# First x tiles in column pieces, their transposes packed into fewer PSUM tiles, merged late loads and a shorter warm-up, in a fused two-layer kernel on one core

## Chip, core and metric

The kernel runs on one core of a Trainium2 chip. The metric is device time in microseconds (us), as the median of several executions.

## The reference

```python
# B, S, D, F = 1, 2048, 576, 4608, all bf16
def reference(x, w1, b1, w2, b2):
    h = jnp.einsum("bsd,df->bsf", x, w1) + b1
    zero = jnp.zeros_like(h)
    r = jnp.where(h > zero, h, zero)
    h = r * r
    out = jnp.einsum("bsf,fd->bsd", h, w2) + b2
    return out
```

## The kernel before

x is worked off in four blocks of 512 rows. For the first layer PE needs x transposed. Blocks 1 to 3 get that from transposing DMAs; block 0 cannot wait for those, so its four row tiles (128 rows each) are loaded as they are and transposed on PE, 128 columns at a time, against an identity, into PSUM. DVE and ACT copy the results to SBUF (`xT0`). The first four output tiles of layer one are computed chunk by chunk of w1 (`part`), while the rest loads. Meanwhile PE runs a few warm-up matmuls on constants, because its clock starts at half rate (shown below).

The parts that matter (cuts marked):

```python
    wps = ps_o.tile([P, 512], FP32, name="wps", tag="po")
    WARM = [512] * 6 + [128]
    # ... one matmul for each width in WARM

    load_x(nc.sync, 0)        # a whole row tile: 128 x 576
    load_x(nc.scalar, 1)
    load_w1n(nc.sync, 0)      # w1 rows 0..127, columns 0..511
    load_x(nc.scalar, 2)
    load_w1n(nc.sync, 1)
    load_x(nc.sync, 3)
    for k in range(2, NK):
        load_w1n(nc.sync, k)
    # ... b1 and part of b2 are loaded from the gpsimd queue

    tb_po = [ps_o.tile([P, 2, HS], BF16, name="tb", tag="po") for _ in range(2)]
    tb_ph = [ps_h.tile([P, 2, HS], BF16, name="tb", tag="ph") for _ in range(4)]
    # x_transpose(j, k): one 128x128 transpose of row tile j, column chunk k,
    # each k of a half (two row tiles) into a PSUM tile of its own
    # x_copies(h): five copies of half h, on DVE and ACT in turn

    # ... in a_full(0, "k_outer"):
                for j in range(2):
                    for k in range(NK):
                        x_transpose(j, k)
                for j in range(2):
                    x_transpose(j, NK)
                x_copies(0)
                part(0, 0)
                for k in range(NK + 1):
                    x_transpose(2, k)
                part(0, 1)
                part(0, 2)
                for k in range(NK + 1):
                    x_transpose(3, k)
                x_copies(1)
                dup_windows(0)
                part(0, 3)
                part(1, 0)
                make_b1T()
                for k in range(1, NK):
                    part(1, k)
    # ... then two pairs of 64-row matmuls, and the long stage a_rows(0), which
    # takes w1 in column chunks j0..j1:
    for (j0, j1) in [(0, 1), (1, 2), (2, 4), (4, 6), (6, 8), (8, 10), (10, 12)]:
        load_w1(nc.sync, 0, j0, j1)
        load_w1(nc.sync, 1, j0, j1)
        # ...
    load_xT(1)
    for (j0, j1) in [(12, 14), (14, 16)]:
        load_w1(nc.sync, 0, j0, j1)
        load_w1(nc.sync, 1, j0, j1)
```

## Time and profile before

| | before |
|---|---|
| median at first / range | 291.28 us / 291.16 to 291.34 (3 runs) |
| span of the profiled execution | 289.6 us |
| PE busy | 285.5 us, 99% |
| opening: start of the first 64-row pair (timeline) | 9.85 us |

The first line of the profile's page for the kernel before gives busy time, share of the span and number of instructions for each engine.

```profile
PE 285.5 (99%) x2027; PEld 139.9 (48%) x2032; DVE 78.6 (27%) x176; ACT 96.7 (33%) x154; POOL 2.3 (1%) x10
```

PE is the limit, and only its opening has slack. The timeline of PE in the opening of the kernel before, with start, length, line, operation, count and, in brackets, idle time and what ended it:

```profile
2.86 0.74 PE L63 MATMUL wps<-const-bfloat16-1.0 128*128 128x512 bf16 x2
3.77 1.25 PE L149 MATMUL tb<-ident,x_sb 128*128 128x128 bf16 x10 [0.17 <-DMA x_sb<-in_x_dram]
4.87 1.01 PE L227 MATMUL pn<-xTw,w1n 128*128 128x256 bf16 x4
5.68 0.74 PE L149 MATMUL tb<-ident,x_sb 128*128 128x128 bf16 x5
6.21 1.19 PE L227 MATMUL pn<-xTw,w1n 128*128 128x256 bf16 x8
7.24 0.44 PE L149 MATMUL tb<-ident,x_sb 128*128 128x128 bf16 x5
...
9.85 0.39 PE L203 MATMUL pn<-xTw,w1n 64*128 64x512 bf16 x1
```

Two things are to be seen. First, PE waits once, 0.17 us, for x. Second, five transposes take 0.74 us at 5.68 and 0.44 at 7.24: the clock doubles in between. The records of single matmuls put the step at 6.51 us; start to start, a transpose takes 107 ns before it and 56 after, a matmul of 256 columns 213 and 109. (The record of a transpose, 311 ns in the first of these groups, is longer than the distance of starts, so records overlap; the distance is what counts.)

The table of stretches of the kernel before, for 2 to 4 and 4 to 6 us; the last two columns are the DMA engines' busy share and GB/s:

```profile
core 0: us, PE busy (x) PEld busy (x) DVE busy (x) ACT busy (x) POOL busy (x), PEclk, DMA share, GB/s
2.00:4.00 2.00, 1.83 (x8) 0.68 (x7) 0.00 (x0) 1.15 (x2) 0.70 (x2) 1.00 0.96 314
4.00:6.00 2.00, 2.00 (x18) 1.73 (x16) 0.78 (x3) 0.65 (x2) 0.18 (x1) 1.00 0.92 247
```

So 0.63 MB (314 GB/s times 2 us) arrive from 2 to 4 us, while PE warms up.

### The profile page before, as it was taken

The numbers are of one execution on the slowest core, as the hardware profiler recorded it, in microseconds if no ns is written. First come the engines' busy times: TensorE is split into PE (matmuls) and PEld (weight loads), VectorE is DVE, ScalarE is ACT, GpSimd is POOL, SyncE is SP. The second block draws the span as 40 slices with busy tenths as digits, with TensorE's granted clock in tenths as the row PEclk, the third lists the DMA queues.
The fourth block names the chain that finished last, engine by engine and source line by source line (L and its number), as shares of the span: only waits on it lengthen the run. The fifth ranks groups of instructions, "written<-read, shape, count | busy, mean of one in ns | idle before, by whom it ended". The sixth has DMA issues, their size and how long they took to land.

```text
span 289.6 us, 4693 instructions
## 1 busy us (share of the span) xinstructions
PE 285.5 (99%) x2027; PEld 139.9 (48%) x2032; DVE 78.6 (27%) x176; ACT 96.7 (33%) x154; POOL 2.3 (1%) x10
## 2 busy tenths in 40 slices
PE   8999999999999999999999999999999999999996
PEld 5544444444444555555544444444444455555555
DVE  1644554444500200000015444444440001100001
ACT  2566666666500000000027666666670000000000
POOL 3000000000000000000000000000000000000000
PEclk9999999999999999999999999999999999999999
DMA  7999999400001200000000000000000110000000
GB/s 198 221 245 188 308 389 212 92 0 2 0 14 25 52 16 18 16 16 18 16 16 2 1 2 0 2 0 2 0 2 0 36 38 16 16 16 19 33 16 18
DMA packets 31605, 16.52 MB, mean 57 GB/s; under 512 B 15700, under 2 KB 31584, under 8 KB 31584
## 3 DMA queue, kind: packets, MB, share of 16 engines
q1 hardware_dynamic: 31232, 15.91, 22.3%
q10 hardware_dynamic: 288, 0.30, 0.4%
q8 instruction: 16, 0.26, 0.4%
q14 instruction: 5, 0.04, 0.0%
q0 software_dynamic: 64, 0.01, 0.0%
HBM read 11.36 MB, written 2.36 MB: 47 GB/s over the span
## 4 chain that ended last, share of the span: by engine, by line
PE 98%; DMA 1%; issue 0%; DVE 0%
PE ph L188 42%; PE po L289 38%; PE pt L270 11%; PE pn L209 4%; PE pn L227 1%; DMA x_sb<-in_x_dram 1%; PE tb L149 1%; PE ph L190 1%; PE pn L203 1%; DVE o_sb L291 0%; PE b1T_ps L166 0%; PE pn L205 0%
## 5 line engine op out<-in xcount | busy, mean ns | idle before, releaser
L190 PE MATMUL ph<-xTw,w_h 64*128 64x512 bf16 x576 | 124.6, 376 | 0.0
L188 PE MATMUL ph<-xTw,w_h 64*128 64x512 bf16 x576 | 124.6, 376 | 0.0
L289 PE MATMUL po<-w_sb,hT 128*128 128x448 bf16 (+2 forms) x612 | 109.4, 341 | 0.0
L176 ACT ACTIVATE r<-ph,b1T 128x512 bf16<-128x512 f32 x128 | 81.1, 685 | 41.6 <-PE ph L190 41.6
L188 PEld LDWEIGHTS <-w_h 64*128 64x128 bf16 x576 | 54.1, 94 | 68.3
L289 PEld LDWEIGHTS <-hT 128*128 128x128 bf16 x612 | 58.5, 98 | 51.0
L177 DVE TENSOR_TENSOR hT<-r 128x512 bf16<-128x512 bf16 x144 | 61.2, 426 | 75.9 <-ACT r L176 75.5
L190 PEld LDWEIGHTS <-w_h 64*128 64x128 bf16 x576 | 54.1, 94 | 0.0
L291 DVE TENSOR_TENSOR o_sb<-po,b_bc 128x448 bf16<-128x448 f32 (+2 forms) x17 | 10.2, 597 | 125.8 <-PE po L289 125.8
L270 PE MATMUL pt<-hT,w_sb 128*128 128x512 bf16 x142 | 31.3, 379 | 0.1
L176 ACT ACTIVATE r<-pn,b1T 128x512 bf16<-128x512 f32 x16 | 10.3, 688 | 61.0 <-PE pn L205 59.6
L270 PEld LDWEIGHTS <-w_sb 128*128 128x128 bf16 x144 | 14.1, 98 | 17.0
L273 ACT ACTIVATE oT<-pt,b2T 128x512 bf16<-128x512 f32 x4 | 2.8, 688 | 28.3 <-PE pt L270 28.3
L209 PE MATMUL pn<-xTw,w1n 128*128 128x512 bf16 x45 | 10.4, 379 | 0.4 <-issue 0.3
L209 PEld LDWEIGHTS <-w1n 128*128 128x128 bf16 x48 | 4.5, 98 | 6.0 <-issue 0.8
L227 PE MATMUL pn<-xTw,w1n 128*128 128x256 bf16 x32 | 4.6, 295 | 0.0
L63 PE MATMUL wps<-const-bfloat16-1.0 128*128 128x512 bf16 (+1 forms) x7 | 2.8, 582 | 0.8 <-PEq L344 0.8
L227 PEld LDWEIGHTS <-w1n 128*128 128x128 bf16 x32 | 3.3, 107 | 0.5
L156 DVE COPY xTw<-tb 128x256 bf16<-128x256 bf16 x4 | 1.1, 292 | 6.7 <-PE tb L149 6.7
L119 DVE COPY xTw<-xTw 64x2048 bf16<-64x2048 bf16 x4 | 2.8, 690 | 0.2
L120 DVE COPY xTw<-xTw 64x2048 bf16<-64x2048 bf16 x4 | 2.7, 687 | 0.1
L149 PE MATMUL tb<-ident,x_sb 128*128 128x128 bf16 x20 | 2.4, 288 | 0.2 <-DMA x_sb<-in_x_dram 0.2
(23 smaller groups left out, 15.2 us busy)
## 6 DMA issues: line engine op xcount, KB each, us to landing
w_sb<-in_w_dram SPq DMA_DIRECT2D x4, 1296.0 KB, 12.7
w_h<-in_w_dram SPq DMA_DIRECT2D x14, 288.0 KB, 6.2
out_dram<-o_sb SPq DMA_DIRECT2D x15, 112.0 KB, 1.7
w_h<-in_w_dram SPq DMA_DIRECT2D x4, 144.0 KB, 3.5
w1n<-in_w_dram SPq DMA_DIRECT2D x4, 128.0 KB, 3.9
out_dram<-ot SPq DMA_DIRECT2D x4, 128.0 KB, 2.0
x_sb<-in_x_dram ACTq DMA_DIRECT2D x2, 144.0 KB, 2.9
x_sb<-in_x_dram SPq DMA_DIRECT2D x2, 144.0 KB, 3.4
```

The lines of the kernel that those rows point to most:

```text
L63: keep(nc.tensor.matmul(wps[:, 0:n], lhsT=ones[:, 0:P], rhs=ones[:, 0:n], start=True, stop=True))
L149: keep(nc.tensor.transpose(bank[:, slot, qc], xs[:, j, c0:c0 + P], ident[:]))
L176: keep(nc.scalar.activation(out=r[:], in_=bank[:], func=ACT.Relu, bias=b1T[:, ft:ft + 1], scale=1.0))
L177: keep(nc.vector.tensor_tensor(out=hTs[sb][:, ft, :], in0=r[:], in1=r[:], op=ALU.mult))
L188: keep(nc.tensor.matmul(bx[:], lhsT=w1_h[0:H, LO_C[i], jc], rhs=xT[0:H, LO_W[i], :], start=(i == 0), stop=(i == NC - 1)))
L190: keep(nc.tensor.matmul(by[:], lhsT=w1_h[H:P, UP_C[i], jc], rhs=xT[H:P, UP_W[i], :], start=(i == 0), stop=(i == NC - 1)))
L203: keep(nc.tensor.matmul(banks[2 * i][:], lhsT=w1n8[0:H, i, :], rhs=xT[0:H, SPC, :], start=start, stop=stop, skip_group_check=order == "k_o ...
L209: keep(nc.tensor.matmul(banks[g][:], lhsT=w1n[:, k, g * P:(g + 1) * P], rhs=xT[:, O + k, :], start=start, stop=stop))
L227: keep(nc.tensor.matmul(banks[g][:, hc], lhsT=w1n[:, k, g * P:(g + 1) * P], rhs=xT[:, O + k, hc], start=(h == 0 and k == 0), stop=False, s ...
L270: keep(nc.tensor.matmul(pt[:], lhsT=w2_sb[:, ft, DM:D], rhs=hT[:, ft, :], start=(i == 0), stop=(i == NFT - 1)))
L289: keep(nc.tensor.matmul(po[:, 0:d1 - d0], lhsT=hT[:, ft, jj * P:(jj + 1) * P], rhs=w2_sb[:, ft, d0:d1], start=(i == 0), stop=(i == NFT - 1)))
L291: keep(nc.vector.tensor_tensor(out=o_sb[:, d0:d1], in0=po[:, 0:d1 - d0], in1=b2_bc[:, d0:d1], op=ALU.add))
```

## The change

The intent: let transposes begin as soon as 256 columns of x are there, feed the rest in the order in which it is used, and shorten the warm-up accordingly. Along with it, the five transposes of a half are packed into two PSUM tiles, each is copied out as soon as its second row tile is done, b1 and b2 leave the gpsimd queue, and late loads are merged. Its core:

```diff
-    WARM = [512] * 6 + [128]
+    WARM = [512] * 5 + [256]
...
-    load_x(nc.sync, 0)
-    load_x(nc.scalar, 1)
-    load_w1n(nc.sync, 0)
-    load_x(nc.scalar, 2)
-    load_w1n(nc.sync, 1)
-    load_x(nc.sync, 3)
-    for k in range(2, NK):
-        load_w1n(nc.sync, k)
+    for c0, c1 in [(0, 2 * P), (2 * P, D)]:
+        load_x(nc.sync, 0, c0, c1)
+        load_x(nc.scalar, 1, c0, c1)
+    for k in range(2):
+        load_w1n(nc.sync, k, k + 1)
+        load_x(nc.scalar, 2 + k)
+    load_w1n(nc.sync, 2, 3)
+    load_w1n(nc.scalar, 3, 4)
...
-    W2CH = 9
+    W2CH = 18
...
+    tb = [[ps_h.tile([P, 4, HS], BF16, name="tb", tag="ph") for _ in range(2)] for _ in range(2)]
+    PLACE = [(0, 0), (0, 1), (1, 0), (1, 1), (0, 2)]
+    T_ORDER = [0, 1, 2, 3, NK]
+    def x_transpose(j, ks=T_ORDER):
         h, q = divmod(j, 2)
+        for k in ks:
+            bank, slot = PLACE[k]
+            c0 = k * P if k < NK else D - P
+            keep(nc.tensor.transpose(tb[h][bank][:, slot, q * P:(q + 1) * P], xs[:, j, c0:c0 + P], ident[:]))
+            if q == 1:
+                w = O + k if k < NK else E3
+                if h == 1 and bank == 1:
+                    keep(nc.scalar.copy(out=xT0[:, w, hc], in_=tb[h][bank][:, slot, :]))
+                else:
+                    keep(nc.vector.tensor_copy(out=xT0[:, w, hc], in_=tb[h][bank][:, slot, :]))
...
+                for ks in (T_ORDER[:2], T_ORDER[2:]):
+                    for j in range(2):
+                        x_transpose(j, ks)
+                for k in range(2):
+                    part(0, k)
+                    x_transpose(2 + k)
                 dup_windows(0)
+                for k in range(2, NK):
+                    part(0, k)
...
-    for (j0, j1) in [(12, 14), (14, 16)]:
+    for (j0, j1) in [(12, 16)]:
```

Cut: b1 and b2 loads, the layout of a small w1 remainder, and the first output banks, which move to the other PSUM pool.

More of the change, by code (lines that the diff above doesn't have):

```diff
@@ L57 @@
     ps_o = ctx.enter_context(tc.tile_pool(name="ps_o", bufs=4, space=PSUM))
-    wps = ps_o.tile([P, 512], FP32, name="wps", tag="po")
+    wps = ps_h.tile([P, 512], FP32, name="wps", tag="ph")
     ones = nc.const_aps.tensor(1.0, [P, 512], BF16)
-    WARM = [512] * 6 + [128]
+    WARM = [512] * 5 + [256]
     for i, n in enumerate(WARM):
@@ L66, with load_x, load_w1n @@
     w1n = wpool.tile([P, NK, GW], BF16, name="w1n")
-    w1n8 = wpool.tile([P, G // 2, P], BF16, name="w1n8")
+    w1n8 = wpool.tile([P, GW], BF16, name="w1n8")
     w1_h = wpool.tile([P, NC, FH], BF16, name="w1_h")
     w1_v = w1.rearrange("(c p) f -> p c f", p=H)
-    def load_x(eng, rt):
-        keep(eng.dma_start(out=xs[:, rt, :], in_=x2[rt * P:(rt + 1) * P, :]))
-    def load_w1n(eng, k):
-        keep(eng.dma_start(out=w1n[:, k, :], in_=w1[k * P:(k + 1) * P, 0:GW]))
+    def load_x(eng, rt, c0=0, c1=D):
+        keep(eng.dma_start(out=xs[:, rt, c0:c1], in_=x2[rt * P:(rt + 1) * P, c0:c1]))
+    def load_w1n(eng, k0, k1):
+        src = w1[k0 * P:k1 * P, 0:GW].rearrange("(k p) f -> p k f", p=P)
+        keep(eng.dma_start(out=w1n[:, k0:k1, :], in_=src))
     def load_w1n8(eng, h):
-        src = w1[NK * P:D, 0:GW].rearrange("p (i h f) -> p i h f", h=2, f=P)
-        keep(eng.dma_start(out=w1n8[h * H:(h + 1) * H, :, :], in_=src[:, :, h, :]))
+        keep(eng.dma_start(out=w1n8[h * H:(h + 1) * H, :], in_=w1[NK * P:D, 0:GW]))
     def load_w1(eng, h, j0, j1):
@@ L83, in load_w1 @@
                       in_=w1_v[:, :, GW + h * FH + j0 * P:GW + h * FH + j1 * P]))
-    load_x(nc.sync, 0)
-    load_x(nc.scalar, 1)
-    load_w1n(nc.sync, 0)
-    load_x(nc.scalar, 2)
-    load_w1n(nc.sync, 1)
-    load_x(nc.sync, 3)
-    for k in range(2, NK):
-        load_w1n(nc.sync, k)
+    b1_rows = const.tile([P, P], BF16, name="b1_rows")
+    nc.vector.memset(b1_rows[:], 0.0)
+    for c0, c1 in [(0, 2 * P), (2 * P, D)]:
[6 more added lines that the diff above has]
+    load_w1n(nc.scalar, 3, 4)
     ident = const.tile([P, P], BF16, name="ident")
     make_identity(nc, ident[:])
-    b1_rows = const.tile([P, P], BF16, name="b1_rows")
-    nc.gpsimd.memset(b1_rows[:], 0.0)
-    nc.gpsimd.dma_start(out=b1_rows[0:NFT, :], in_=b1.rearrange("(ft p) -> ft p", p=P))
-    b2_col = const.tile([P, 1], BF16, name="b2_col")
-    nc.gpsimd.dma_start(out=b2_col[:], in_=b2[DM:D].rearrange("(d o) -> d o", o=1))
-    b2T = const.tile([P, 1], FP32, name="b2T")
-    nc.gpsimd.tensor_copy(out=b2T[:], in_=b2_col[:])
     warm = const.tile([P, 1], FP32, name="warm")
     keep(nc.scalar.activation(out=warm[:], in_=nc.const_aps.tensor(0.0, [P, 1], FP32), func=ACT.Relu))
+    keep(nc.scalar.dma_start(out=b1_rows[0:NFT, :], in_=b1.rearrange("(ft p) -> ft p", p=P)))
+    for h in range(2):
+        load_w1n8(nc.sync, h)
     E3, O, SPC, E = 0, 1, 5, 6
@@ L140 @@
     HS = SB // 2
-    tb_po = [ps_o.tile([P, 2, HS], BF16, name="tb", tag="po") for _ in range(2)]
-    tb_ph = [ps_h.tile([P, 2, HS], BF16, name="tb", tag="ph") for _ in range(4)]
-    half_banks = [tb_ph, None]
-    def x_transpose(j, k):
+    tb = [[ps_h.tile([P, 4, HS], BF16, name="tb", tag="ph") for _ in range(2)] for _ in range(2)]
+    PLACE = [(0, 0), (0, 1), (1, 0), (1, 1), (0, 2)]
+    T_ORDER = [0, 1, 2, 3, NK]
+    def x_transpose(j, ks=T_ORDER):
         h, q = divmod(j, 2)
-        qc = slice(q * P, (q + 1) * P)
-        bank, slot, c0 = (half_banks[h][k], 0, k * P) if k < NK else (half_banks[h][2], 1, D - P)
-        keep(nc.tensor.transpose(bank[:, slot, qc], xs[:, j, c0:c0 + P], ident[:]))
-    def x_copies(h):
         hc = slice(h * HS, (h + 1) * HS)
-        for k in range(NK):
-            src = half_banks[h][k][:, 0, :]
-            if k % 2 == 0:
-                keep(nc.vector.tensor_copy(out=xT0[:, O + k, hc], in_=src))
-            else:
-                keep(nc.scalar.copy(out=xT0[:, O + k, hc], in_=src))
-        keep(nc.vector.tensor_copy(out=xT0[:, E3, hc], in_=half_banks[h][2][:, 1, :]))
+        for k in ks:
[8 more added lines that the diff above has]
+                    keep(nc.vector.tensor_copy(out=xT0[:, w, hc], in_=tb[h][bank][:, slot, :]))
     b1T = const.tile([P, NFT], FP32, name="b1T")
     def make_b1T():
-        b1T_ps = ps_o.tile([P, P], BF16, name="b1T_ps", tag="po")
+        b1T_ps = ps_h.tile([P, P], BF16, name="b1T_ps", tag="ph")
         keep(nc.tensor.transpose(b1T_ps[:], b1_rows[:], ident[:]))
@@ L198, in a_full @@
         for g in range(G):
-            pool, tag = (ps_o, "po") if g < 2 else (ps_h, "ph")
+            pool, tag = (ps_o, "po") if g < 2 or order == "k_outer" else (ps_h, "ph")
             banks.append(pool.tile([P, SB], FP32, name="pn", tag=tag))
         def pair(i, start, stop):
-            keep(nc.tensor.matmul(banks[2 * i][:], lhsT=w1n8[0:H, i, :], rhs=xT[0:H, SPC, :],
+            keep(nc.tensor.matmul(banks[2 * i][:], lhsT=w1n8[0:H, 2 * i * P:(2 * i + 1) * P], rhs=xT[0:H, SPC, :],
                              start=start, stop=stop, skip_group_check=order == "k_outer"))
-            keep(nc.tensor.matmul(banks[2 * i + 1][:], lhsT=w1n8[H:P, i, :], rhs=xT[H:P, E3, :],
+            keep(nc.tensor.matmul(banks[2 * i + 1][:], lhsT=w1n8[H:P, (2 * i + 1) * P:(2 * i + 2) * P], rhs=xT[H:P, E3, :],
                              start=start, stop=stop, skip_group_check=order == "k_outer"))
@@ L220, in a_full @@
             if order == "k_outer":
-                tb_new = [ps_h.tile([P, 2, HS], BF16, name="tb", tag="ph") for _ in range(2)]
-                half_banks[1] = tb_new + tb_po
                 def part(h, k):
@@ L229, in part @@
                                               skip_group_check=True))
-                for j in range(2):
-                    for k in range(NK):
-                        x_transpose(j, k)
-                for j in range(2):
-                    x_transpose(j, NK)
-                x_copies(0)
-                part(0, 0)
-                for k in range(NK + 1):
-                    x_transpose(2, k)
-                part(0, 1)
-                part(0, 2)
-                for k in range(NK + 1):
-                    x_transpose(3, k)
-                x_copies(1)
+                for ks in (T_ORDER[:2], T_ORDER[2:]):
[4 more added lines that the diff above has]
+                    x_transpose(2 + k)
                 dup_windows(0)
-                part(0, 3)
+                for k in range(2, NK):
+                    part(0, k)
                 part(1, 0)
@@ L296 @@
         load_w1(nc.sync, 1, j0, j1)
-        if j0 == 0:
-            load_w1n8(nc.sync, 0)
-            load_w1n8(nc.sync, 1)
     load_xT(1)
-    for (j0, j1) in [(12, 14), (14, 16)]:
+    for (j0, j1) in [(12, 16)]:
         load_w1(nc.sync, 0, j0, j1)
         load_w1(nc.sync, 1, j0, j1)
+    b2_col = const.tile([P, 1], BF16, name="b2_col")
+    keep(nc.sync.dma_start(out=b2_col[:], in_=b2[DM:D].rearrange("(d o) -> d o", o=1)))
+    b2T = const.tile([P, 1], FP32, name="b2T")
+    nc.gpsimd.tensor_copy(out=b2T[:], in_=b2_col[:])
     keep(nc.sync.dma_start(out=b2_bc[:], in_=b2.partition_broadcast(P)))
-    for c in (0, 2, 1, 3):
+    for c in range(2):
         load_w2(c)
```

## The prediction

> **What bounds the kernel now.** PE: 285.5 us busy of a span of 289.6 (99%) on the page; the chain of waits is 98% PE. Between 10 and 286 us it idles under 0.5 us (table of stretches). Only the opening can pay, and the change touches only that: it ends at 9.85 us, where the first 64-row pairs start.
>
> **The opening before, from the timeline.** Seven warm-up matmuls run from 0.78 to 3.60. The first x tiles land at 3.52 (ACT queue) and 3.73 (sync queue); transposes start at 3.77. Then PE hardly stops until 9.75. Its work is 20 transposes, 32 matmuls of 256 columns and the b1 transpose. Start to start these take 107 and 213 ns until 6.5 us, then 56 and 109 ns: the granted clock doubles at 6.51. At the fast rate the work is 20x0.056 + 32x0.109 + 0.056 = 4.67 us. The Trainium skill, "TensorE: Matmul & The Clock Gate", section "What's actually happening", gives half rate until one busy window of about 3.4 us has passed; this trace agrees in kind, with the step 5.7 us after the first matmul. It calls the window free-running; the runs of before (291.16 to 291.34) spread far less than a wandering window would give, so I expect the same moment after the change.
>
> **What the change does.**
> - x tiles 0 and 1 come as 256 + 320 columns on two queues: about 128 KB before the first transposes instead of 288. Packets of 1152, 1024 and 768 bytes took 51, 46 and 36 ns, so I estimate 26 for 512 bytes: landing near 3.1 to 3.3 us.
> - The warm-up shrinks by 0.5 us, ending near 3.1. Transposes start at 3.15 to 3.3, some 0.5 us earlier.
> - After four transposes (0.43 us) the second pieces are needed, near 3.65; they land near 3.75: a wait of 0.1 to 0.2. w1 chunk 0 is issued 0.45 us later with the same bytes ahead of it; it landed at 4.32 and should at 4.3 to 4.5, when the ten transposes end.
> - Two small loads leave the gpsimd queue; the DMA rate fell to 211 GB/s at 4 to 5 us while they ran. w1 chunk 1 (landed 5.86) should come no later.
> - b1 is issued from ACT after five loads and the 1.28 us table load, near 4.5; landing at 6.3 to 7.5, needed at about 8.1. Tight, but enough.
> - The first half's five copies all go to DVE (0.29 us each), hidden behind PE. The first block's banks move to the other pool; w2 and late w1 chunks merge: nothing waits for them before or after.
>
> **On the critical path.** Everything gained lies before 6.51 us, at half clock, so 0.4 us of earlier work is worth 0.2. With a start at 3.2 and 0.15 us of waits, (6.51-3.2-0.15)/2 = 1.58 us of fast-rate work is done by the step, 3.09 left: parts end near 9.6 instead of 9.75. Gain 0.1 to 0.3 us, about 0.06%.
>
> **Predicted time:** 291.1 us, 8 in 10 between 290.3 and 291.6. Faster by over 2%: 0.005; within 2%: 0.99; slower: 0.005.
>
> **What would show it.** Timeline: first transposes at 3.15 to 3.3; a short wait for the second x pieces; the clock's step still near 6.5; the pairs at 9.6 to 9.75; everything later the same but shifted. PE busy falls by about 0.5 us of warm-up, no gain by itself.
>
> **What would make it wrong.** The shorter warm-up plus new waits leave the decisive window too idle, and the fast clock comes a window (3.4 us) later: 1.7 us worse. Or the step comes earlier, for up to 1.7 us better. b1 landing after 8.1 us would stall PE one for one. Leaving the gpsimd queue unused may change the 1.7 us outside the span.

## The result, and the profile after

The changed kernel took 292.24 us (median of 6, 292.17 to 292.63); the kernel before, over its 6 runs, 291.24. The ratio is 1.0038, with a 95% interval of 1.0026 to 1.0051. Ratios here are the mean time of one kernel's fast runs over that of the other's of the same rounds, so not quite the ratio of the medians quoted. A gain of 0.2 us was predicted; the change lost 1.0 us, where the stated range ended at 291.6 us.

The first line of the page and the timeline of PE in the opening, of the changed kernel:

```profile
PE 285.1 (98%) x2031; PEld 139.2 (48%) x2031; DVE 79.3 (27%) x179; ACT 96.0 (33%) x152; POOL 1.0 (0%) x7
```

```profile
2.43 0.85 PE L63 MATMUL wps<-const-bfloat16-1.0 128*128 128x512 bf16 x2
3.07 0.53 PE L149 MATMUL tb<-ident,x_sb 128*128 128x128 bf16 x3
3.98 0.33 PE L149 MATMUL tb<-ident,x_sb 128*128 128x128 bf16 x3 [0.38 <-DVE xTw L155]
4.58 0.27 PE L149 MATMUL tb<-ident,x_sb 128*128 128x128 bf16 x2 [0.27 <-DVE xTw L155]
5.24 0.27 PE L149 MATMUL tb<-ident,x_sb 128*128 128x128 bf16 x2 [0.38 <-DVE xTw L155]
...
6.50 0.22 PE L149 MATMUL tb<-ident,x_sb 128*128 128x128 bf16 x1
7.10 0.27 PE L149 MATMUL tb<-ident,x_sb 128*128 128x128 bf16 x2 [0.38 <-DVE xTw L155]
7.83 0.27 PE L149 MATMUL tb<-ident,x_sb 128*128 128x128 bf16 x2 [0.46 <-ACT xTw L153]
...
10.71 0.39 PE L198 MATMUL pn<-xTw,w1n 64*128 64x512 bf16 x1
```

The list of PE's waits over the whole changed kernel says the same; the kernel before has no entry for a copy there:

```profile
PE tb L149 <- DVE xTw L155: 1.4, 4, 0.4
PE tb L149 <- ACT xTw L153: 0.5, 1, 0.5
```

Transposes do start earlier: 3.07 against 3.77 us. But five of them wait for a copy. From the records of single matmuls, the five distances of starts are 0.695, 0.489, 0.599, 0.601 and 0.677 us where 0.107 (at half clock) or 0.055 would do, which is 2.7 us of standing still. The pairs start at 10.71 us instead of 9.85. And this profiled execution was lucky with its clock: the step came at 3.59 us, not 6.51.

The distances of starts add up. From the first transpose to the first pair the kernel before took 6.08 us: 4.66 us is the same work at the fast distances, 1.3 what the distances at half clock add, 0.1 standing still. The changed kernel took 7.64 us: 4.66, 0.2 and 2.8. (Distances of up to about double the fast one are counted as half clock, longer ones as standing.) So in this execution the waits for copies are the whole loss. It began 0.70 us earlier, stood 2.7 us longer and saved 1.1 by the earlier step, which makes 0.9; the pairs came 0.86 us later.

The DMA engines, in the table of stretches of the changed kernel:

```profile
2.00:4.00 2.00, 1.62 (x8) 0.78 (x7) 0.29 (x1) 0.52 (x1) 0.00 (x0) 1.00 0.88 215
4.00:6.00 2.00, 1.35 (x15) 1.06 (x15) 1.07 (x4) 0.96 (x2) 0.00 (x0) 1.00 0.95 325
```

Only 0.43 MB arrive from 2 to 4 us, a third less than before. So there are two suspects, and the early clock step, a third matter, hides part of their cost. Loads that come late might have held PE up had the copies not done so.

### The profile page after: what moved, and what is told of

The parts are those of the page before. It is cut to its first block, busy times and chain, and to the rows that moved or that the text cites. A ratio compares the mean times of both kernels' runs of the same rounds, so it can differ in the third digit from the quotient of the medians.

```text
span 290.4 us, 4694 instructions
## 1 busy us (share of the span) xinstructions
PE 285.1 (98%) x2031; PEld 139.2 (48%) x2031; DVE 79.3 (27%) x179; ACT 96.0 (33%) x152; POOL 1.0 (0%) x7
## 4 chain that ended last, share of the span: by engine, by line
PE 98%; DVE 1%; issue 0%; ACT 0%
PE ph L183 42%; PE po L274 38%; PE pt L255 11%; PE pn L204 4%; PE pn L219 1%; PE wps L63 1%; PE tb L149 1%; PE ph L185 1%; PE pn L198 1%; DVE xTw L155 0%; ACT xTw L153 0%; DVE o_sb L276 0%; PE b1T_ps L161 0%; PE pn L200 0%
## 5 line engine op out<-in xcount | busy, mean ns | idle before, releaser
L219 PE MATMUL pn<-xTw,w1n 128*128 128x256 bf16 x32 | 4.0, 272 | 0.0
L155 DVE COPY xTw<-tb 128x256 bf16<-128x256 bf16 x8 | 2.2, 290 | 5.3 <-PE tb L149 5.3
L149 PEld LDWEIGHTS <-x_sb 128*128 128x128 bf16 x20 | 1.7, 105 | 3.0 <-issue 1.6
L117 DVE COPY xTw<-xTw 64x2048 bf16<-64x2048 bf16 x4 | 2.8, 689 | 0.2
```

What stands on the lines that cost most here:

```text
L149: keep(nc.tensor.transpose(tb[h][bank][:, slot, q * P:(q + 1) * P], xs[:, j, c0:c0 + P], ident[:]))
L219: keep(nc.tensor.matmul(banks[g][:, hc], lhsT=w1n[:, k, g * P:(g + 1) * P], rhs=xT[:, O + k, hc], start=(h == 0 and k == 0), stop=False, s ...
```

## The experiments

All kernels below gave correct results. "Ratio" is against the kernel before on the same chip in the same rounds. Its own median was 290.86, 291.10, 290.96 and 290.78 us.

### 1. Copies batched, so that no transpose waits for one

```diff
-    PLACE = [(0, 0), (0, 1), (1, 0), (1, 1), (0, 2)]
+    PLACE = [(0, 0), (0, 1), (1, 0), (1, 1), (1, 2)]
...   all transposes of a call first, then its copies
-            if q == 1:
-                # copy of this k
+        if q == 1:
+            for k in ks:
+                # copy of each k
```

Expected:

> Theory W (bank waits): the changed kernel lost about 2.7 us to PE standing still at five transposes, each held until a copy that reads another slot of the same PSUM tile had ended. Here each group's transposes are all issued before its copies, and the fifth transpose of a row tile moves to the second bank; loads, pieces, warm-up and pools stay. W expects the five waits (0.4 to 0.6 us each) to be gone from PE's list of waits, the pairs to start at 9.0 to 9.9 us instead of 10.71, and 290.4 to 291.4 us: at or a little under the kernel before. Rival L (loads): the loads in pieces deliver late, and the waits only show where PE would have stood anyway; L expects PE to wait for x and w1 by the same amount and 292.0 to 292.4 us.

Measured: 291.97 us (291.24 to 292.93), ratio 1.0041. W is right that the five waits go, and wrong on the time. L's time (from 292.0) is missed by 0.03 us, and PE does wait for x and w1, though for far less than L expected. PE now waits elsewhere, as the timeline and PE's weight-load waits of this run show:

```profile
3.07 1.46 PE L149 MATMUL tb<-ident,x_sb 128*128 128x128 bf16 x10
5.11 1.04 PE L221 MATMUL pn<-xTw,w1n 128*128 128x256 bf16 x4 [0.58 <-DVE xTw L157]
```

```profile
PEld L221 <- DMA w1n<-in_w_dram: 0.8, 1, 0.8
PEld L149 <- DMA x_sb<-in_x_dram: 0.6, 2, 0.3
```

The first `part` starts at 5.11 us, later than the 4.87 of the kernel before, although its transposes began 0.7 us earlier. The line blames DVE, but the copy of the chunk that this matmul reads had ended at 4.03; the weight load ahead of it waited 0.8 us for w1 chunk 0. Behind the waits for copies stood a second limit, the loads.

But in this execution the clock stepped at 8.88 us. By the account above, the stretch to the first pair is 8.07 us: 4.66 of work, 1.1 standing (2.8 in the changed kernel) and 2.3 that the half clock adds (0.2 there). So here the later step, more than the loads, took back what the repair had won. The six executions fall into two groups, 291.2 to 291.5 and 292.4 to 292.9 us; the profiled one is of the second. That the clock parts the groups is not shown, as the others were not traced.

### 2. The new loads alone, in the kernel before

> The kernel before with only the new loads (pieces, alternation, b1 and b2 off the gpsimd queue, merged chunks); old warm-up, old transposes, old banks. W expects no loss: 290.6 to 291.4 us, within 0.15% of the kernel before. L expects most of the loss here: 291.9 to 292.4 us.

Measured: 292.32 us (291.74 to 292.67), ratio 1.0052. L's range (291.9 to 292.4) holds, and theory W fails here as the only cause: the loads by themselves cost about as much as the whole change (the intervals, 1.0038 to 1.0066 and 1.0026 to 1.0051, overlap). Its trace moved 253 GB/s from 2 to 4 us. This run is not pure, though: in the old structure ACT makes some of the first half's copies, and with the new loads ACT first issues five loads and b1, so a copy came late too (0.4 us of PE's waits).

### 3. The changed kernel with the old, longer warm-up

> The changed kernel with the old warm-up (six of 512 columns and one of 128). Rival C (clock): the shorter warm-up leaves PE less busy and delays the fast clock in most runs; C expects 291.2 to 291.6 us here. W expects no gain: the chain of transposes and copies just starts about 0.5 us later, of which the wait for the second x pieces takes up 0.3 or so; 292.2 to 292.8 us, the same five waits in the list.

Measured: 292.48 us; five runs within 0.02 us and one of 295.84; ratio 1.0076 (1.0056 without that one). W's range holds. The shorter warm-up as such is not what costs. The outlier, 3.4 us longer, could come from a later clock step; its trace was not kept, so that is not shown.

### 4. The new transposes and banks alone, in the kernel before

> The kernel before with only the new transposes and banks; old loads and old warm-up. W expects the whole loss or more: transposes start at 3.77 as before and then wait five times for copies; 292.2 to 293.0 us. L and C expect the time of the kernel before, 291.0 to 291.5 us.

Measured: 294.12 us (292.57 to 295.76), ratio 1.0114: alone, the new transposes lose three times what the whole change lost, and more than W expected. Its profiled execution, of 295.67 us, shows the clock's share. The lines are from its timeline:

```profile
9.80 2.77 PE L221 MATMUL pn<-xTw,w1n 128*128 128x256 bf16 x12
12.36 0.31 PE L163 MATMUL b1T_ps<-ident,b_rows 128*128 128x128 bf16 x1
```

Twelve matmuls of 256 columns in 2.77 us are still at half rate. Start to start they took 213 ns until 13.0 us and 109 from there. PE had stood five times before. By the account above, standing cost 3.0 us and the half clock another 3.0 (1.3 in the kernel before). Whether the idle time kept the clock down, or chance did, no run separates.

### 5 and 6. Whole x tiles again, with the rest of the change kept

Run 5 is run 1, and run 6 is run 2, with this edit:

```diff
-    for c0, c1 in [(0, 2 * P), (2 * P, D)]:
-        load_x(nc.sync, 0, c0, c1)
-        load_x(nc.scalar, 1, c0, c1)
+    load_x(nc.sync, 0)
+    load_x(nc.scalar, 1)
```

> The first batch showed that neither half alone accounts for the loss, and that the fast clock's step moves between runs (3.6 to over 10 us). Theory B (both): two limits stand side by side in the opening, the five transposes that wait for copies, and loads that deliver later because x tiles 0 and 1 in pieces leave the DMA engines short of work at 2 to 4 us (0.43 MB moved against 0.63 in the kernel before). Undoing one leaves the other. This is the changed kernel with batched copies and with tiles 0 and 1 as whole loads; all else of the change stays. B expects 290.4 to 291.3 us, within 0.15% of the kernel before. Rival O (order): the alternation of w1 chunks and x on two queues is what is late, not the pieces; O expects 291.4 to 292.6 us, as in the run with batched copies alone.

> The kernel before with the new loads, but tiles 0 and 1 whole. B expects the loss of the loads alone (1.4 us) to be mostly gone: 290.5 to 291.4 us, with about 0.6 MB moved at 2 to 4 us. O expects 291.7 to 292.6 us.

Measured: 291.65 us, ratio 1.0019, and 291.66 us, ratio 1.0024. About half of the loss went away in each (from 1.0041 and 1.0052; the intervals overlap), and 292 and 294 GB/s moved from 2 to 4 us, nearly the old rate. Both still missed B's range, and run 5 lies in that of the rival O, which blames the alternation of w1 and x on two queues. O is settled only by run 10, which keeps the alternation and has no loss left. A further cost stood. In run 5 the opening was over at 9.65 us, earlier than in the kernel before, yet its span was 0.3 us longer. The records of single matmuls show where: one step of 0.45 us instead of 0.21 at 33.9 us in run 5, and one of 0.67 at 34.2 in run 6, at the first matmul of the merged w1 chunk of columns 12 to 16. (In run 6 one matmul also waited 0.6 us for a copy on ACT, as in run 2.)

### 7, 8 and 9. The opening moved late, so that neither loads nor clock matter

Three kernels, the changed one, the one of run 1 and the one before, each got `WARM = [512] * 28`. They are slower by design; what is read is the stretch from the first transpose to the first 64-row pair.

> The changed kernel with 28 warm-up matmuls, so that transposes begin after all first loads have landed and after the fast clock was granted: what the chain of transposes and copies costs by itself. Longer in total by design; what is read is the stretch from the first transpose to the first 64-row pair. B expects 7.0 to 7.4 us there (4.8 us of work at the fast rate and five waits of 0.4 to 0.6 us). Rivals that blame loads or clock expect 4.8 to 5.3 us.

> The kernel before with the same 28 warm-up matmuls, for comparison: its transposes go four to six to a pool and its copies follow in a block, so PE should wait once or twice for a copy at most. First transpose to first pair: 4.8 to 5.6 us.

> The changed kernel with batched copies and 28 warm-up matmuls: the twin of the run that held the changed transposes late. There the stretch from first transpose to first 64-row pair took 7.44 us (kernel before: 5.03). If the waits for copies are the whole of that difference, this takes 4.9 to 5.3 us; if something else in the new banks or order costs, it stays above 6.

The timeline of the changed kernel held late:

```profile
9.79 0.33 PE L149 MATMUL tb<-ident,x_sb 128*128 128x128 bf16 x3
10.50 0.33 PE L149 MATMUL tb<-ident,x_sb 128*128 128x128 bf16 x3 [0.38 <-DVE xTw L155]
11.10 0.27 PE L149 MATMUL tb<-ident,x_sb 128*128 128x128 bf16 x2 [0.27 <-DVE xTw L155]
11.75 0.27 PE L149 MATMUL tb<-ident,x_sb 128*128 128x128 bf16 x2 [0.38 <-DVE xTw L155]
...
17.23 0.39 PE L198 MATMUL pn<-xTw,w1n 64*128 64x512 bf16 x1
```

And that of its twin with batched copies:

```profile
8.97 0.72 PE L149 MATMUL tb<-ident,x_sb 128*128 128x128 bf16 x10
9.74 0.60 PE L221 MATMUL pn<-xTw,w1n 128*128 128x256 bf16 x4
...
13.94 0.39 PE L200 MATMUL pn<-xTw,w1n 64*128 64x512 bf16 x1
```

And that of the kernel before, held late:

```profile
9.69 0.72 PE L149 MATMUL tb<-ident,x_sb 128*128 128x128 bf16 x10
14.71 0.39 PE L203 MATMUL pn<-xTw,w1n 64*128 64x512 bf16 x1
```

The stretch is 17.23 - 9.79 = 7.44 us in the changed kernel, 13.94 - 8.97 = 4.97 with batched copies and 14.71 - 9.69 = 5.02 in the kernel before. PE's list of waits names no DMA in these stretches, and the clock was fast in all three. So the waits for copies cost 2.47 us by themselves, and the new banks and order cost nothing else. Each of the three ran once, so its state is unknown; but the distances of starts are those of the fast clock, and with loads and clock out of the way there is little left for executions to differ by.

### 10. Run 5 with the merged chunks in two again

```diff
-    W2CH = 18
+    W2CH = 9
...
-    for (j0, j1) in [(12, 16)]:
+    for (j0, j1) in [(12, 14), (14, 16)]:
```

> The run with batched copies and whole x tiles still lost 0.55 us; its trace shows PE standing 0.24 us longer than a step at 33.9 us, where the merged chunk of columns 12 to 16 lands at 33.81. Theory M (merged chunk): its landing is a third limit, which the slow opening of the changed kernel hid. Here the chunk is in two pairs of loads again, and w2 in four. M expects 290.9 to 291.4 us, within 0.1% of the kernel before, and no stop near 34 us. If the rest is in the opening, it stays at 291.5 to 291.8.

Measured: 291.05 us, ratio 1.0007 (0.9994 to 1.0020): the time of the kernel before, with the new alternation, banks, shorter warm-up and b1 and b2 off the gpsimd queue all kept. No step over 0.3 us is left near 34 us in its trace.

### 11. The merged chunks alone, in the kernel before (labelled e12)

> The kernel before with only the merged chunks (columns 12 to 16 in one pair of loads, w2 in two). M expects a stop at the thirteenth column block, near 33 us, of 0.3 to 1.2 us: 291.3 to 292.2 us. If merging is free, as the prediction held: 290.6 to 291.4.

Measured: 291.85 us, ratio 1.0031 (1.0017 to 1.0044). Its list of PE's waits from 30 to 36 us has two lines that the kernel before has not:

```profile
PEld L190 <- DMA w_h<-in_w_dram: 0.7, 1, 0.7
PE ph L190 <- DMA w_h<-in_w_dram: 0.2, 1, 0.2
```

The second half of the merged chunk landed at 33.83 us and was wanted at 33.5; in the kernel before, the second half of columns 12 to 14 landed at 30.54.

### 12. Run 10 with six whole warm-up matmuls (labelled e13)

> Candidate for the best: as the run with the chunk in two pairs, but six warm-up matmuls of 512 columns, so that PE has no gap before the whole x tiles land at 3.4 to 3.6 us. Expected 290.7 to 291.3 us: within 0.1% of the kernel before, perhaps a little under it, because PE's busy share in the first windows is higher and b1 and b2 no longer share the DMA engines at 4 to 5 us.

Measured: 291.15 us, ratio 1.0006 (0.9994 to 1.0018). It is the same as run 10 and as the kernel before. No version beat the kernel before.

### 13 and 14. The column pieces by themselves (labelled e14 and e15)

Run 13 is run 10 with the pieces back; run 14 is the kernel before with only the pieces.

> The version with batched copies, whole tiles and two pairs of chunks measured 1.0007 of the kernel before; here x tiles 0 and 1 come in column pieces again, nothing else differs. Theory P (pieces starve the loads): w1 chunk 0 lands about 0.4 us later, PE stands once or twice, and the idle time can push the fast clock's step out by a window in some runs: ratio 1.002 to 1.005, 291.6 to 292.6 us with a wide spread. If pieces are harmless once copies are batched: 1.000 to 1.001.

> The kernel before with its tiles 0 and 1 in the two column pieces, nothing else changed (w1 chunk 0 is then issued third on its queue). P expects less than 0.58 MB moved from 2 to 4 us (0.63 before), the first tile whole later, and a ratio of 1.001 to 1.004. The intent of the change would be right if it came to 0.998 to 1.000.

Run 14 measured 291.70 us (291.53 to 291.73), ratio 1.0029 (1.0016 to 1.0042), as theory P expected. Its table of stretches, and the waits of PE's weight loads in its opening:

```profile
2.00:4.00 2.00, 1.81 (x7) 0.71 (x5) 0.00 (x0) 1.49 (x2) 0.69 (x2) 1.00 0.97 211
```

```profile
PEld L228 <- DMA w1n<-in_w_dram: 0.7, 2, 0.4
PEld L150 <- DMA x_sb<-in_x_dram: 0.6, 1, 0.6
```

The first pieces landed at 2.70 and 2.87 us, as the change intended, but the second ones at 3.94 and 4.14, and w1 chunk 0 at 5.26 instead of 4.32. Transposes started 0.38 us earlier and then stood; standing comes to 1.2 us in all. In this profile the clock stepped at about 5.4 us, and so its pairs start at 9.80, no later than the 9.85 of the kernel before: the cost is shown by the times, not by this one opening.

Run 13 measured, in its five fast runs, 291.17 to 293.66 us, ratio 1.0072; theory P expected up to 1.005, so it cost more than expected. A sixth, the profiled one, took 433.95 us at a mean granted clock of 0.658 and counts as slow; as its trace is of no use for the clock, why the others spread over 2.5 us is argued from run 4, not shown.

## Why the prediction was wrong

**What held.** PE bounds the kernel and only the opening moves. The first pieces landed at 2.93 and 3.09 us (predicted 3.1 to 3.3) and transposes began at 3.07 (3.15 to 3.3), both a little earlier still; b1 came in time, and gpsimd's small loads out of the way did no harm.

**The step that failed first** reads "The first half's five copies all go to DVE (0.29 us each), hidden behind PE." They were not hidden. A copy of one slot and the next transpose into another slot of the same PSUM tile took turns: transpose, 0.2 to 0.3 us until its record ends, 0.29 us of copy, next transpose. Priced at nothing, these turns left PE standing 2.7 us in the changed kernel. The late twins show 2.47 us for five such turns, and 0 with the copies behind all transposes of their group. The Trainium skill, "PSUM — Partial Sum Buffer", section "PSUM bank collisions raise a hardware error", says that a PE write and a copy may not touch one bank and quadrant (32 partitions) at one time and that PSUM is to be guarded "by bank × quadrant", "not by address". The traces agree as far as they can: PE waits although the slots differ. I costed the copies by their length and their engine's idle time, and did not ask which transposes share a bank with them. In the trace each of these five transposes carries a wait for a semaphore that a copy on DVE or ACT raises. So the waits were in the program, and reading its list of waits would have shown them before anything ran.

**The second** reads "w1 chunk 0 is issued 0.45 us later with the same bytes ahead of it; it landed at 4.32 and should at 4.3 to 4.5". The bytes ahead were the same, but they moved at 215 GB/s from 2 to 4 us instead of 314. With the pieces alone chunk 0 landed at 5.26, a term of 0.9 us that I had put at 0.1. (The trace of the changed kernel does not tell chunk 0's landing; its second pieces landed at 3.94 and 4.13, predicted near 3.75.) I priced pieces by the packet (26 ns estimated for 512 bytes; 27 measured for most). For most packets that was right, but not for the mean: the 256 packets of 640 bytes took 32 ns at the median and 41 on average in the changed kernel, 53 in run 14, with single ones up to 0.9 us. In the kernel before, those of 1152 bytes took 54 on average from 2 to 4 us. The Trainium skill, "DMA: Bandwidth & Descriptors", section "Rules for kernel authors", advises to coalesce small transfers because under 64 KB overhead dominates; here pieces of 64 and 80 KB already cost 0.29%. That the pieces cost it is shown by run 14; why the bytes moved more slowly stays open. Slow issue is an obvious suspect, as each of the first eight loads of the changed kernel held its queue for 0.40 to 0.47 us, whatever its size. But two queues can then still hand out 2 x 72 KB per 0.45 us, about 320 GB/s (an estimate from those numbers), more than what moved in either kernel; six loads of 560 KB had been issued by 2.1 us, of which only 0.47 MB had moved by 4 us; and the DMA engines' busy share in run 14 was 0.97, no lower than the 0.96 before.

**The third** reads "w2 and late w1 chunks merge: nothing waits for them before or after." PE waits for a merged load as a whole. Alone in the kernel before it costs 0.31%. In the profile of the changed kernel no such wait shows: its opening was 0.9 us later, so PE came to the chunk later. Besides, the second of its two loads landed at 32.43 us there, before even the kernel before would have wanted it; in runs 1 to 3, 5, 6 and 11 it landed at 33.15 to 34.15. Why it came earlier is open.

**The clock.** I wrote "I expect the same moment after the change", on the ground that three runs agreed. The step came at 6.51 us in the kernel before, at 3.59 in the changed one, and in the experiments between 4.17 and 8.88, and at 13.0 in run 4. The Trainium skill, "TensorE: Matmul & The Clock Gate", section "What's actually happening", calls the window free-running, and these traces agree (runs 7 to 9, alike for PE until 8.9 us, had it at 6.74, 5.06 and 6.5 us); I should have kept to the page. Three close times showed only that the time depended little on the step's moment in those three. So the predicted arithmetic of half-rate work until 6.51 us had no ground. The stated alternative, that idle time could push the fast clock out, is what runs 1 and 4 fit; run 14, which stood 0.9 us before its step, got it at about 5.4, so idle time alone does not decide. That the changed kernel's step came as early as 3.59 was luck as far as the runs tell, and without it the loss would have been larger.

**Why the parts do not add up.** The first two costs are limits side by side on one short stretch, the clock works on both, and the merged chunk bites later, near 34 us. Alone: transposes 1.14%, pieces 0.29%, merged chunk 0.31%. Together 0.38%, which is argued from the profiles and not tested: PE standing for a copy lets loads land, a late opening leaves a late chunk more time, and in its profile the half clock added 1.1 us less than in the kernel before. That is also why the first repair gained nothing: run 1 took one limit away and met the next, with a clock step 5.3 us later on top. Only with all three undone did the time return (run 10). The large figure for the transposes alone is in part the clock: in its profile the half clock added 1.7 us more than in the kernel before. Its executions, with spans of 290.8, 292.3 and 293.9 us, fall into groups about 1.5 us apart; that the clock parts these too is not shown.

What stays open: how busy a window must be for the fast clock, why pieces move more slowly, and the spread of run 13.

## What to carry to other kernels

When results are packed into fewer PSUM banks, issue all writes to a bank before the first read of it, and read the built program's list of waits before costing anything. Splitting the first loads brought the first bytes earlier and what was wanted next later (w1 chunk 0 by 0.9 us in run 14): compare the bytes moved in the first microseconds, not only the first landing. If undoing one suspect gains nothing, look for a second limit behind it before acquitting the suspect, and see first whether both profiles had the fast clock from the same moment.

## What the Trainium skill lacked or had wrong

- "TensorE: Matmul & The Clock Gate" puts the step about 4 us into sustained work, give or take 0.5. With unbroken matmuls from 0.77 us on (runs 7, 8 and 9) it came at 6.74, 5.06 and 6.5 us, so 4.3 to 6.0 us into the work; with gaps as late as 13.0 us (run 4). No page says how busy a window must be.
- The same page, section "Part 4: PE-mode transpose", says that the full clock does not engage for transposes. Here their distance of starts fell from 107 to 56 ns at the step, like that of other matmuls. Whether they count as busy work towards the step, no run here tells.
- "DMA: Bandwidth & Descriptors", section "Issuing engines are not separate DMA queues", calls the time saved by issuing from several engines "usually small relative to the DMA itself". Here one issue of the first eight held the sync or scalar queue for 0.40 to 0.47 us; its 64 to 144 KB need 0.2 to 0.5 us at the 314 GB/s measured (an estimate).
- The same page's rule to coalesce does not name the price, that the first bytes wanted are waited for with all the others: merging columns 12 to 16 into one pair of loads moved the landing of the pair that holds columns 12 and 13 from 30.54 to 33.83 us and cost 0.31%.
